# Moving the score and output steps of a fused retention and feed-forward kernel along TensorE's order, and one copy to VectorE

## The chip, the cores and the metric

The kernel runs on one core of a Trainium2 chip. The metric is the device time of one execution in microseconds (us). The profile's names for the engines are kept: PE is TensorE (PEld its weight loads), DVE is VectorE, ACT is ScalarE, POOL is GpSimdE, SP is SyncE, which issues nearly all DMAs. PEclk is the clock that TensorE was granted, 1.00 being full speed.

## The reference: what is computed

Retention for 8 batches, 8 heads, 576 positions and a head size of 64, and then a feed-forward block with a tanh Gelu on the 4608 tokens of 512 features that it gives. Inputs and output are float32.

```python
scores = q @ k.transpose(0, 1, 3, 2) / sqrt(64)
gamma  = 1 - 2.0 ** (-5 - arange(8))            # one decay for each head
rel    = pos[:, None] - pos[None, :]
ret    = scores * where(rel >= 0, gamma ** rel, 0)
x      = (ret @ v).transpose(0, 2, 1, 3).reshape(4608, 512)
h      = x @ w_in                                # 512 x 2048
out    = gelu_tanh(h) @ w_out                    # 2048 x 512
```

## The kernel before

**The work.** The decay is split into a factor for the query's position and one for the key's, applied when q and k are cast to float16 (lines 262 to 297, mostly on GpSimdE). Each batch is cut into four chunks of 128 positions and a tail of 64. Within a chunk the scores are matmuls (`score`, L430) that VectorE masks from PSUM to SBUF (`masks`, L440, its operation at L444). Between chunks a state, k transposed times v (`state`, L454), is summed on VectorE (`scan_halves`, operations at L494, L477 and L472) and cast by ScalarE into the tiles `tbb` and `tbt` (L497 and L505). An output (`outputs`, L526) is the masked scores times v plus the queries times the state. `put` (L561) then copies it, on ScalarE (L569), into `xT`, the feed-forward block's transposed input. The scores and outputs are made of 64x64 matmuls, four of them side by side in the array (`pack`, L401); each has a weight load of its own.

**Blocks.** The feed-forward block runs over nine blocks of 512 tokens, block t for batch t and the ninth for the tails. A block from the third on first multiplies with w_in (`up`, L577, 16 times four matmuls of 128x512, L583, each group followed by a Gelu on ScalarE, L589), and then with w_out: seven products (`prod`, L751, matmuls of 128x256 at L768) in the manner of Strassen, whose sums VectorE and ScalarE take from PSUM (`after`, L775, operations at L782, L821 and L838). Blocks 0 and 1 take their w_in products in halves (L604), and block 1 has these before its own units.

**The order.** The kernel is scheduled by hand. Inside the loop over blocks t, the retention work of batch t + 1 is put between the feed-forward steps. `at(t, u, f)` hangs f behind unit u of block t, and the engines' queues get their instructions in the order in which the steps are then called. In blocks 1 to 7 units 0 to 15 are the w_in steps and units 16 to 29 are the products, two for each (one per half u), in the order 1, 6, 5, 7, 2, 4, 3. Each product is 16 matmuls, 8 for each half. Their PSUM tiles are opA (products 1 and 2), opB (6, 7 and 4) and opC (5 and 3).

The lines that the change touches stand in the planner (L1046 to L1062):

```python
U2 = (21, 23, 28)
at(1, 16, lambda: pack([state(2, 0)]))
...
    s0, o0, o1 = U2 if t == 1 else (11 if t in (2, 3, 4) else 9, 15, 24)
    at(t, s0, lambda b=b, tl=tl: scores(b, tl))
    at(t, o0, lambda b=b, tl=tl: outs(b, 0, tl, (b, 1) if b < B else None))
...
    at(t, o1, lambda b=b: outs(b, 1, None, (b + 1, 0) if b + 1 < B else None))
```

`scores` makes the scores of both halves of batch t + 1, 64 matmuls (and 16 for a pair of tails in blocks 3, 4, 6 and 7), and the four masks. `outs(b, 0)` makes the first half's outputs and, between two changes of the array's use (`TURN`, one small matmul each), the states of the second half; `put` follows in the same step. `outs(b, 1)` makes the second half's outputs and the first states of the batch after. `later` (units 25 and 26 in block 1) hangs the sums of those states on VectorE and their casts on ScalarE. So in block 1 the scores of batch 2 stand between products 5 and 7, the first outputs between products 7 and 2, and the second outputs in the middle of product 3; block 2 follows with its w_in products, which read `xT`.

**PSUM.** There are eight banks, handed out first in, first out by `bank` and `drop` (L61 to L69). The scores hold four, an output step four and one more for the array's changes.

**DMA.** SyncE issues the loads of q, k and v into 16 buffers (`pump`), the stores, and the transposes of the cast k and q into `tt` (L324), which the scores and outputs read. The transposes of a batch stand behind its last cast of q, one block ahead of their use.

Of the kernel before, what the change touches and what calls it, by code (L numbers as in the profile page):

```python
# [20 lines left out]
def kernel(  # L21
# [9 lines left out]
    nc = tc.nc  # L31
# [12 lines left out]
    NPE = 2  # L44
# [22 lines left out]
    def drop(t):  # L67
        spare.append(home.pop(id(t))[0])
# [332 lines left out]
    def pack(*phases, n=None):  # L401
        opened = set()
        for phase in phases:
            if phase is TURN:
                t = ps.tile([128, 512], F32, tag=f"p{n}", name="turn", bufs=1)
                nc.tensor.matmul(t[0:64, 0:4], ident[0:64, 0:64], ident[0:64, 0:4], start=True, stop=True)
                continue
            todo = {x: deque() for x in TILES}
            for jobs in phase:
                for x, *job in jobs:  # L410
                    todo[x].append(job)
            done = dict.fromkeys(TILES, 0)
            while any(todo.values()):
                x = min((x for x in TILES if todo[x]), key=lambda x: done[x])
                t, out, lhsT, rhs = todo[x].popleft()
                k = (id(t), x[1])
                if len(rhs.shape) == 3:
                    out = out.rearrange("p (j t) -> p j t", j=2)
                nc.tensor.matmul(out, lhsT, rhs, start=k not in opened, stop=True, skip_group_check=True)  # L419
                opened.add(k)  # L420
                done[x] += 1
        if n is not None:
            spare.append(n)
# [30 lines left out]
    def state(b, g):  # L454
        a = att[b]
        us = [bank("us") for _ in range(2)]
        out = []
        for o in range(2):
            c = 2 * g + o
            a["U", c] = (us, o)  # L460
            for p in range(HP):
                for r in range(2):
                    i = 256 * o + 64 * p
                    for h in range(2):
                        out.append((
                            (h, r), us[h], us[h][hv(r), i : i + 64], a["k"][hv(h), col(c, p, r)], a["v"][hv(h), col(c, p, row(p, r))]
                        ))
        return out
# [91 lines left out]

    def put(b, g):  # L561
        for h, t in enumerate(att[b].pop(("xs", g))):
            if b >= PAIR:
                nc.scalar.copy(
                    out=xT[:, GM + b - PAIR + h], in_=t.rearrange("p (n x t) -> p n x t", n=HP, x=2)[:, :, 0]
                )
            else:
                g0 = 8 * (b % 2) + 4 * g + h
                nc.scalar.copy(  # L569
                    out=xT[:, g0 : g0 + 4 : 2].rearrange("p g n (t j) -> p g n j t", j=2),  # L570
                    in_=t.rearrange("p (n g j t) -> p g n j t", n=HP, g=2, j=2),
                )
            drop(t)
# [313 lines left out]
    def later(b, c):  # L887
        (scan if b < NPE else scan_halves)(b, c)
        spread(b, c, A.copy)
# [53 lines left out]
    def at(t, u, f, last=False):  # L943
        events.setdefault((t, u, last), []).append(f)
# [75 lines left out]
    def scores(b, tails=None):  # L1020
        w = [score(b, g) for g in range(2)] if b < B else []
        if tails is not None:
            w.append(score(PAIR + tails, 0))
        pack(w)
        if b < B:
            masks(b, 0), masks(b, 1)
        if tails is not None:
            masks(PAIR + tails, 0)

    def outs(b, g, tails=None, ahead=None):  # L1030
        n = spare.popleft()
        first, second, between, todo = [], [], [], []
        if b < B:
            todo.append((b, g))
        if tails is not None:
            todo.append((PAIR + tails, 0))
        for x in todo:
            early, late = outputs(*x)
            first.append(early), second.append(late)
        if ahead is not None:  # L1040
            between.append(state(*ahead))
        pack(first, TURN, between, TURN, second, n=n)
        for x in todo:
            put(*x)

    U2 = (21, 23, 28)  # L1046
    at(1, 16, lambda: pack([state(2, 0)]))
    for c in range(2):
        at(1, 17 + c, lambda c=c: later(2, c))
    for t in range(1, B):  # L1050
        b, tl = t + 1, TP.get(t)
        s0, o0, o1 = U2 if t == 1 else (11 if t in (2, 3, 4) else 9, 15, 24)
        at(t, s0, lambda b=b, tl=tl: scores(b, tl))
        at(t, o0, lambda b=b, tl=tl: outs(b, 0, tl, (b, 1) if b < B else None))
        if b == B:
            continue
        at(t, 25 if t == 1 else 16, lambda b=b: later(b, 2))
        at(t, 26 if t == 1 else 20, lambda b=b: later(b, 3))
        at(t, o1, lambda b=b: outs(b, 1, None, (b + 1, 0) if b + 1 < B else None))
        if b + 1 < B:  # L1060
            for c in range(2):
                at(t + 1, c, lambda c=c, nb=b + 1: later(nb, c))  # L1062
# [119 lines left out]
```

## Time and profile before

| What | Value |
| --- | --- |
| Median of 3 runs | 290.66 us (288.53 to 291.45) |
| The profiled execution | 292.24 us |
| Its span, first to last instruction | 290.5 us |
| Mean granted TensorE clock in it | 0.991 |
| TensorE busy | 275.9 us, 95% |
| VectorE / ScalarE / GpSimdE busy | 195.9 / 169.4 / 114.6 us |
| Read and written in HBM | 36.70 and 9.44 MB |

A line of the timeline gives the start, the time from the first start to the last end of a run of equal instructions, the engine, the line, the operation with the tile that it writes and those that it reads, and how many there are; in brackets the idle time before it and what ended that. Matmuls overlap, so the time of a run reaches a little into the next one: the start of the next run tells better how long one took. "issue" as a cause means that the engine waited for nothing that the profile shows. The columns of a row of stretches are, in this order, the stretch, its length, busy time and (x count) of PE, PEld, DVE, ACT and POOL, the granted clock, the DMA engines' share, and GB/s.

### The profile page before, as it was taken

What the parts mean: (1) busy time and instruction counts of PE and PEld (TensorE: products, weight loads), DVE (VectorE), ACT (ScalarE), POOL (GpSimd) and SP (SyncE); (2) the same over time, 40 slices, a digit from 0 to 9 for tenths busy, and PEclk for the clock granted to TensorE, in tenths of its full rate; (3) what the DMA queues carried; (4) which work ended last, traced back from release to release, by engine and by line L of the source; (5) the groups of instructions that cost most, each with busy time, mean ns of one, the idle gap of its engine ahead of it and who ended that gap; (6) DMA issues with size and microseconds to landing.
All of it is one profiled execution on the core that took longest, in us unless ns stands there. A gap on an engine that the chain in (4) does not pass through costs nothing.

```text
span 290.5 us, 9420 instructions
## 1 busy us (share of the span) xinstructions
PE 275.9 (95%) x3986; PEld 202.8 (70%) x3986; DVE 195.9 (67%) x411; ACT 169.4 (58%) x327; POOL 114.6 (39%) x225
## 2 busy tenths in 40 slices
PE   6789998999799999999999999999999999999993
PEld 2458876888574488548854785478547887887782
DVE  6787988677816573667366746753687867975863
ACT  5387755996237674667466755675566358507800
POOL 4589769971780059205920490049330000000000
PEclk9999999999979999999999999999999999999998
DMA  7999999989979994998999929996982030003013
GB/s 198 305 375 367 380 289 262 278 216 202 237 147 246 248 210 103 224 261 193 197 207 267 208 73 220 260 221 136 234 201 39 2 146 2 2 28 119 0 38 108
DMA packets 127306, 54.09 MB, mean 186 GB/s; under 512 B 93472, under 2 KB 119072, under 8 KB 127264
## 3 DMA queue, kind: packets, MB, share of 16 engines
q1 hardware_dynamic: 126672, 52.97, 78.0%
q8 instruction: 31, 0.51, 0.8%
q10 hardware_dynamic: 592, 0.52, 0.5%
q14 instruction: 11, 0.09, 0.1%
HBM read 36.70 MB, written 9.44 MB: 159 GB/s over the span
## 4 chain that ended last, share of the span: by engine, by line
PE 79%; DMA 10%; POOL 4%; DVE 2%; SPq 1%; issue 1%; ACT 1%; POOLq 0%
PE hp L583 26%; PE opB L768 13%; PE opA L768 10%; PE opC L768 8%; PE hp L604 5%; DMA ld<-in_q_dram 4%; DMA ld<-in_moe_w_out_dram 4%; PE hB L677 3%; PE xs L419 3%; DMA ld<-in_moe_w_in_dram 2%; POOL cq L283 2%; PE hC L677 2%; PE st L419 2%; POOL ck L283 1%; PE us L419 1%; PE opD L768 1%
## 5 line engine op out<-in xcount | busy, mean ns | idle before, releaser
L583 PE MATMUL hp<-xT,w_in_sb 128*128 128x512 f16 x352 | 79.0, 379 | 0.5 <-ACT xT L569 0.5
L589 ACT ACTIVATE gT<-hp 128x512 f16<-128x512 f32 x88 | 51.1, 598 | 30.2 <-PE hp L583 29.7
L768 PEld LDWEIGHTS <-gT 128*128 128x128 f16 x576 | 55.7, 99 | 11.8 <-issue 3.5
L583 PEld LDWEIGHTS <-w_in_sb 128*128 128x128 f16 x352 | 34.0, 98 | 38.4 <-issue 0.6
L768 PEld LDWEIGHTS <-s 128*128 128x128 f16 x432 | 42.1, 98 | 4.9
L768 PE MATMUL opA<-w_out_sb,gT 128*128 128x256 f16 x288 | 37.1, 276 | 2.7 <-issue 1.9
L294 POOL TENSOR_TENSOR ck<-ld,sc 128x128 f16<-128x128 f32 (+1 forms) x72 | 33.7, 494 | 3.1 <-DMA ld<-in_k_dram 3.0
L745 DVE TENSOR_TENSOR s<-gT 128x512 f16<-128x512 f16 x36 | 16.6, 460 | 23.7 <-ACT gT L589 18.0
L1076 POOL COPY gate<-s 128x1 f16<-128x1 f16 x5 | 0.9, 190 | 77.4 <-DVE s L749 77.4
L275 POOL TENSOR_TENSOR cq<-ld,sc 128x256 f16<-128x256 f32 x48 | 29.8, 639 | 0.2 <-DMA ld<-in_q_dram 0.2
L604 PE MATMUL hp<-xT,w_in_sb 128*128 128x256 f16 x256 | 29.4, 273 | 0.4 <-POOL w_in_sb L874 0.3
L768 PE MATMUL opB<-wt,gT 128*128 128x256 f16 x224 | 27.7, 279 | 0.0
L604 PEld LDWEIGHTS <-w_in_sb 128*128 128x128 f16 x256 | 24.4, 98 | 4.3 <-POOL w_in_sb L874 1.1
L569 ACT CAST xT<-xs 128x512 f16<-128x512 f32 x24 | 15.9, 734 | 19.0 <-PE xs L419 19.0
L782 DVE TENSOR_TENSOR k<-k,opB 128x512 f32<-128x512 f32 x17 | 11.6, 685 | 13.1 <-PE opB L768 11.2
L611 ACT ACTIVATE gT<-hp 128x512 f16<-128x512 f32 x32 | 18.4, 603 | 3.4 <-PE hp L604 3.3
L444 DVE TENSOR_TENSOR ret<-st,cm 128x512 f16<-128x512 f32 x24 | 14.9, 684 | 5.5 <-PE st L419 5.5
L746 DVE TENSOR_TENSOR s<-s,gT 128x512 f16<-128x512 f16 x36 | 16.8, 468 | 1.2
L768 PE MATMUL opB<-wt,s 128*128 128x256 f16 x144 | 17.4, 273 | 0.0
L768 PE MATMUL opC<-wt,s 128*128 128x256 f16 x144 | 17.2, 272 | 0.0
L747 DVE TENSOR_TENSOR gT<-gT 128x512 f16<-128x512 f16 x36 | 16.7, 463 | 0.0
L782 DVE TENSOR_TENSOR ost<-k,opB 128x512 f32<-128x512 f32 x6 | 4.1, 689 | 18.2 <-PE opB L768 18.2
(134 smaller groups left out, 438.9 us busy)
## 6 DMA issues: line engine op xcount, KB each, us to landing
ld<-in_q_dram SPq DMA_DIRECT2D x32, 256.0 KB, 5.4
ld<-in_k_dram SPq DMA_DIRECT2D x32, 256.0 KB, 5.4
ld<-in_v_dram SPq DMA_DIRECT2D x32, 256.0 KB, 5.3
out_dram<-ost SPq DMA_DIRECT2D x16, 512.0 KB, 4.2
ld<-in_moe_w_in_dram SPq DMA_DIRECT2D x16, 256.0 KB, 5.6
ld<-in_moe_w_out_dram SPq DMA_DIRECT2D x16, 256.0 KB, 5.7
lt<-in_k_dram SPq DMA_DIRECT2D x8, 128.0 KB, 5.0
lt<-in_q_dram SPq DMA_DIRECT2D x8, 128.0 KB, 4.2
```

The source lines that it names most:

```text
L275: eng.tensor_tensor(out=a[key][:, 1024 * g + 512 * x : 1024 * g + 512 * x + 512].rearrange("p (n l d) -> p l n d", l=2, d=D)[:, y ^ x], in ...
L294: eng.tensor_tensor(out=dh[:, o], in0=x, in1=sc[:, s0, i].unsqueeze(2).to_broadcast(list(x.shape)), op=ALU.mult)
L419: nc.tensor.matmul(out, lhsT, rhs, start=k not in opened, stop=True, skip_group_check=True)
L569: nc.scalar.copy(out=xT[:, g0 : g0 + 4 : 2].rearrange("p g n (t j) -> p g n j t", j=2), in_=t.rearrange("p (n g j t) -> p g n j t", n=HP, ...
L583: nc.tensor.matmul(hp.rearrange("p (g t) -> p g t", t=TL), w_in_sb[:, ct, 128 * fc : 128 * fc + 128], xT[:, o : o + TB // TL, ct, :], star ...
L589: nc.scalar.activation(out=gT[t][:, fc].rearrange("p i n -> p (i n)"), in_=hp, func=AF.Gelu_apprx_tanh)
L604: nc.tensor.matmul(hps[n][:, 256 * x : 256 * x + 256].rearrange("p (g t) -> p g t", t=TL), w_in_sb[:, ct, 128 * (fs[n] + x) : 128 * (fs[n] ...
L611: nc.scalar.activation(out=gT[t][:, f : f + 2, 2 * u : 2 * u + 2, :].rearrange("p f i n -> p f (i n)"), in_=hp.rearrange("p (f n) -> p f n ...
L745: nc.vector.tensor_tensor(out=s["1"], in0=a21, in1=a22, op=ALU.add)
L746: nc.vector.tensor_tensor(out=s["2"], in0=s["1"], in1=a11, op=ALU.subtract)
L747: nc.vector.tensor_tensor(out=a21, in0=a11, in1=a21, op=ALU.subtract)
L768: nc.tensor.matmul(op[tag][:, HD * u : HD * u + HD], lhs(f), rhs[:, f], start=(new and f == 0), stop=(f == NH - 1), skip_group_check=True,)
```

## The change

Three edits. In block 1 the scores of batch 2 are hung behind unit 19 instead of 21, so they stand between products 6 and 5, and the first outputs behind unit 25 instead of 23, so they stand between products 2 and 4. The second outputs stay in the middle of product 3. In `put`, the copy of the second half of the second outputs of batch 2 into `xT` goes from ScalarE to VectorE. In blocks 2, 3 and 4 the scores are hung behind unit 10 instead of 11.

What follows for the queues: TensorE's instructions are the same 3986 pairs in another order. On VectorE the order of all others stays, with the one copy between the sum that takes product 4 and the one that takes product 3. On ScalarE the copy of opA (L838) now stands ahead of the two copies of the first outputs instead of behind them, and one of the last two copies is gone. GpSimdE's and SyncE's orders stay.

```diff
@@ put(b, g)
         for h, t in enumerate(att[b].pop(("xs", g))):
+            cp = nc.vector.tensor_copy if (b, g, h) == (NPE, 1, 1) else nc.scalar.copy
             if b >= PAIR:
...
                 g0 = 8 * (b % 2) + 4 * g + h
-                nc.scalar.copy(
+                cp(
                     out=xT[:, g0 : g0 + 4 : 2].rearrange("p g n (t j) -> p g n j t", j=2),
                     in_=t.rearrange("p (n g j t) -> p g n j t", n=HP, g=2, j=2),
                 )
@@ the planner
-    U2 = (21, 23, 28)
+    U2 = (19, 25, 28)
...
-        s0, o0, o1 = U2 if t == 1 else (11 if t in (2, 3, 4) else 9, 15, 24)
+        s0, o0, o1 = U2 if t == 1 else (10 if t in (2, 3, 4) else 9, 15, 24)
```

## The prediction

> **What bounds the kernel now.** I read the page first, for engine shares, the clock row and the DMA queues.
>
> ```profile
> span 290.5 us, 9420 instructions
> PE 275.9 (95%) x3986; PEld 202.8 (70%) x3986; DVE 195.9 (67%) x411; ACT 169.4 (58%) x327; POOL 114.6 (39%) x225
> ...
> PEclk9999999999979999999999999999999999999998
> ...
> q8 instruction: 31, 0.51, 0.8%
> ...
> PE 79%; DMA 10%; POOL 4%; DVE 2%; SPq 1%; issue 1%; ACT 1%; POOLq 0%
> ```
>
> TensorE is busy for 95% of the span and is 79% of the chain, so only its pauses and its slow stretches can be won. Its clock dips in one slice before the end, the thirteenth. Queue q8 brings 31 packets of 0.51/31 MB, 16 KB each; TensorE issues 3986 matmuls and 3986 weight loads, 7972 instructions, and 7972/31 is 257. So a packet is a page of some 256 TensorE instructions. Next, TensorE's waits, of which these two lie in block 1, and its stretches around the dip (a row gives the stretch, busy time and count of each engine, then PEclk, DMA share, GB/s):
>
> ```profile
> PE opA L768 <- issue: 1.9, 1, 1.9
> PE hp L583 <- ACT xT L569: 0.5, 1, 0.5
> ```
>
> ```profile
> 43.00:47.00 4.00, 2.79 (x85) 2.11 (x82) 3.21 (x6) 3.44 (x6) 4.00 (x5) 1.00 1.15 287
> 77.85:79.73 1.88, 0.01 (x2) 0.01 (x1) 1.60 (x5) 0.77 (x2) 0.22 (x2) 1.00 1.29 247
> 80.30:83.70 3.40, 3.40 (x19) 2.42 (x17) 0.19 (x1) 1.72 (x5) 3.40 (x8) 0.50 0.73 169
> ```
>
> TensorE stands still for 1.9 us with no engine named, and 0.6 us later runs 3.4 us at half clock. A pause of 1.21 in 4.0 us (first row) cost no clock. Then TensorE's order of time in block 1 and at the start of block 2 (start, us, engine, line, tiles, count, idle before):
>
> ```profile
> 69.82 1.91 PE L768 MATMUL opB<-wt,s 128*128 128x256 f16 x16
> 71.57 1.91 PE L768 MATMUL opC<-wt,s 128*128 128x256 f16 x16
> 73.41 0.74 PE L419 MATMUL st<-tt 64*64 64x64 f16 x64
> ...
> 74.08 1.92 PE L768 MATMUL opB<-wt,gT 128*128 128x256 f16 x16
> 75.93 0.31 PE L419 MATMUL xs<-tt,tbb 64*64 64x64 f16 x12
> ...
> 77.25 0.61 PE L768 MATMUL opA<-w_out_sb,gT 128*128 128x256 f16 x4
> 79.73 2.21 PE L768 MATMUL opA<-w_out_sb,gT 128*128 128x256 f16 x12 [1.87 <-issue]
> 81.73 2.89 PE L768 MATMUL opB<-wt,gT 128*128 128x256 f16 x16
> 84.46 1.04 PE L768 MATMUL opC<-w_out_sb,s 128*128 128x256 f16 x8
> 85.43 0.32 PE L419 MATMUL xs<-tt,tbb 64*64 64x64 f16 x16
> ...
> 86.51 1.05 PE L768 MATMUL opC<-w_out_sb,s 128*128 128x256 f16 x8
> 88.02 10.52 PE L583 MATMUL hp<-xT,w_in_sb 128*128 128x512 f16 x48 [0.46 <-ACT xT L569]
> 98.47 0.74 PE L419 MATMUL st<-tt 64*64 64x64 f16 x64
> ```
>
> The pause falls after four of the sixteen matmuls of one product, whose operands are no different from the first four's: not a wait for data. Last, what moved on the DMA engines in 73.8 to 76.8, 76.8 to 78.2 and 80.8 to 82.5 us:
>
> ```profile
> q1 hardware_dynamic: 2339, 0.72, 130.4%
> ```
>
> ```profile
> q8 instruction: 1, 0.02, 5.7%
> ```
>
> ```profile
> q8 instruction: 1, 0.02, 5.9%
> ```
>
> In the first stretch the data queue takes more than the engines' whole time and no page comes; one comes in 76.8 to 78.2, TensorE resumes 1.5 us after that stretch ends, and the next comes in 80.8 to 82.5. I read the pause as TensorE out of instructions. Small matmuls eat pages fast: the scores are 64 pairs (weight load and matmul), 128 instructions in 74.08 - 73.41 = 0.67 us, and an output step 90 pairs, 180 in 77.25 - 75.93 = 1.32 us, while a product's 32 take 1.75 us. The instruction that waited follows 4 pairs (8), the output step (180) and a product (32), 220 in all; 256 back from it lies 92 instructions into the scores, at 73.41 + 0.67 x 92/128 = 73.9 us. If the page then needed was asked for there, its **latency** was 79.73 - 73.9 = 5.8 us, and TensorE had used up its page by 77.7.
>
> [...]
>
> **The change part by part.** All times are on the clock of this profiled execution: 292.24 us, span 290.5 and 1.74 around it. That is 1.58 over the median of the three runs shown (290.66), 0.79 over the slowest.
>
> *Scores two products forward, outputs one back (block 1).* The same instructions, reordered; SyncE's and GpSimdE's orders stay, so no DMA is passed. TensorE's new order from 71.57: scores 0.67, products 5, 7 and 2 (1.75, 1.75, 1.85 with the 0.1 that precedes a burst), outputs from 77.6 to 78.9, product 4 to 80.7, half of product 3 (84.46 to 85.43 is 0.97) to 81.6, second outputs (1.08) to 82.7, and 0.88 to 83.6. Page edges stay where they are in the count of instructions. The first now comes 124 of 128 into the scores, 71.57 + 0.65 = 72.2; the second 156 of 180 into the outputs, 77.6 + 1.14 = 78.7. Between them are 6.5 us instead of 3.8, more than the latency of 5.8. The pause goes: 79.73 less the 77.69 at which a fifth matmul at 0.11 would have begun, 2.04 us. The half clock goes with it: 12 matmuls took 2.00 and 16 took 2.73, against 1.31 and 1.75, so 1.67 us. **-3.71 us.**
>
> *What is late next.* The third edge comes 184 of 196 into the second outputs, about 82.5, only 3.8 us after the second; by the old order it was 6.6. No row shows a latency so short: the page asked for at 79.73 came by 82.5, and with the 1.5 to resume that is 4.3. The wait is between 0 (latency 3.8) and 2.0 (5.8). I take 4.3, the nearest row, since the DMA share falls from 1.29 to 0.73 just there: **+0.5 us**, too short for a half clock.
>
> The moved steps' own waits, with the rows that hide them:
>
> ```profile
> 64.35 3.10 SPq L324 DMA_TRANSPOSE tt<-cq  x1
> ```
>
> ```profile
> 86.00 3.31 SPq L324 DMA_TRANSPOSE tt<-cq  x1
> ```
>
> ```profile
> DMA to landing us min/median/max: 4.4/5.9/6.5
> ```
>
> ```profile
> 77.30 1.32 ACT L569 CAST xT<-xs 128x512 f16<-128x512 f32 x2 [4.05 <-PE xs L419]
> ...
> 82.46 0.41 ACT L497 CAST tbb<-ts 128x256 f16<-128x256 f32 x1
> 82.77 0.41 ACT L505 CAST tbb<-ws 128x256 f16<-128x256 f32 x1
> 83.07 0.41 ACT L497 CAST tbb<-ts 128x256 f16<-128x256 f32 x1
> ...
> 86.65 1.32 ACT L569 CAST xT<-xs 128x512 f16<-128x512 f32 x2 [2.87 <-PE xs L419]
> ```
>
> ```profile
> 84.66 0.69 DVE L782 TENSOR_TENSOR ost<-k,opB 128x512 f32<-128x512 f32 x1 [4.18 <-PE opB L768]
> 87.59 0.69 DVE L782 TENSOR_TENSOR ost<-k,opC 128x512 f32<-128x512 f32 x1 [2.24 <-PE opC L768]
> ```
>
> The scores need the turned queries: issued at 64.35, landed by 70.9 at the slowest, before 71.57; zero, and every 0.1 us later would be a 0.1 us pause. The second outputs need ScalarE's third state copy. ScalarE now copies opA first (done 78.2), then the outputs (78.9 to 80.2, by the 1.32), then states at 0.31 apart: the third ends at 81.2, TensorE asks at 81.6. Zero, with 0.4 of cover; past that TensorE waits.
>
> *Last copy on VectorE.* TensorE's last matmul of block 1 ends near 86.51 + 0.88 = 87.39 and block 2 begins at 88.02, after ScalarE's two copies in a row (1.32). With one on each engine they end at 86.65 + 0.73, 87.4. VectorE stands idle from 85.35 to 87.59, and its 512-column operations on PSUM take 0.69, so it hides the copy: 0.63 becomes 0.05. From nothing gained (VectorE late) to 0.63; I take **-0.58**. If VectorE were late, the sums of product 3 queue behind it, whose output nobody waits for soon.
>
> *Blocks 2 to 4.* Scores start one unit earlier (four 512-column matmuls: 48 in the 10.45 from 88.02 to 98.47, so 0.87). In block 2 the turned queries, issued at 86.00, land by 92.5 at the slowest; the scores come at 98.47 - 4.3 - 0.87 = 93.3: zero, with 0.8 of cover. No wait of TensorE lies between 88.1 and 285 us other than the one above, and a shorter path to masks that nothing awaits gains nothing. It gives the pages more time, though:
>
> ```profile
> 157.43:162.19 4.76, 4.76 (x152) 2.65 (x140) 4.66 (x11) 2.64 (x5) 0.00 (x0) 1.00 1.32 236
> ```
>
> Counted on from the pause, pages 9 and 10 begin at 157.43 and 162.19, with scores and outputs between: 4.76 us and no pause, but a latency of 5.8 would have cost 1.0. The change adds some 0.8 there. Between 0 and -1.0; zero here, since this execution did not pay it.
>
> *Sum.* 292.24 - 3.71 - 0.58 + 0.5 = 288.4. This execution is 1.58 over the median and over every plain run, which may be a longer pause (not kept) or a cost of recording spread over the span (which the new kernel's plain runs lack too). The fastest plain run, 288.53, is just 292.24 - 3.71: a run without the pause. I split the 1.58 and take half off, 0.8: **287.6 us** for plain runs, and the same 0.8 off each rival.
>
> **The rivals.** *The pause isn't a late page, or stays.* [...] Against: 16 KB per 257 instructions, the packet that ends just before TensorE resumes. Only the copy gains: 292.24 - 0.58 = 291.7 recorded, 290.9 plain.
>
> *The pause moves.* The third edge has 3.8 us, no more than the second had; at the old latency it waits 2.0 and brings the half clock (1.67) again, so 288.4 - 0.5 + 3.7 = 291.6 recorded, 290.8 plain. For it: the near-equal distance. Against: the DMA engines are at 0.73 there, not 1.3.
>
> *Slower: pages come later still.* With latency L the first wait is L - 6.5 and the second L - 3.8, with 1.67 of half clock; together they pass the 4.29 won at 2L = 12.9, L = 6.5. At 7.5 it is 1.0 + 3.7 + 1.67 = 6.4, or 2.1 over the 292.24: 294.3 recorded, 293.5 plain. For it: both requests are now made before 79.7, while the DMA engines are full (130.4% in 73.8 to 76.8). Against: the 5.8 was measured under that very load, and the second request's packet meets the lighter one.
>
> **How the numbers follow.** Pause gone, short or no wait at the next page: 0.65, time 287.6, own range 286.6 to 288.9 (below it no wait, 0.5, and half of the 1.0 of blocks 3 and 4; above it most of the wait's further 1.5). Pause moved in full: 0.15. Pause stays: 0.12. Slower: 0.08, near 293.5. The range reaches from 286.6 to 290.9: it takes in the first three cases and leaves out the slower one and the outer ends of the others. What a measurement of this kernel can tell from no change is about 1%, 2.9 us (the three runs spread over 2.92). Faster by over 1% is below 287.75, somewhat more than half of the first case: 0.40. Slower by over 1%, above 293.57: half of the slow case and a little of the moved pause, 0.06. The rest, 0.54, lies within.
>
> **What would show it.** Right: no "issue" wait of TensorE near 77 to 80, the clock row without its dip, no wait for xT at the start of block 2, which begins near 83.6 to 84.5 instead of 88.02. A wait in the second outputs, just past 82, would be the third edge. Wrong: a half clock elsewhere in block 1, a pause in front of the scores (turned queries late) or of the second outputs (state copies late), or VectorE's copy ending after the last matmul of block 1.

## The result, and the profile after

| What | Before | After |
| --- | --- | --- |
| Median (lowest to highest) of 20 runs each | 290.49 us (288.53 to 292.50) | 288.55 us (287.34 to 291.06) |
| The profiled execution | 292.24 us | 288.71 us |
| Its mean granted TensorE clock | 0.991 | 1.000 |

The changed kernel takes 0.9938 of the time before, with a 95% interval of 0.9915 to 0.9961: between 1.1 and 2.5 us less. That is a gain that can be measured, and it lies within the 1% that the prediction called about the same. A ratio and its interval are worked out from the runs in the faster of two states and not from the medians, so the quotient of two medians can differ from it a little. From here on, the line numbers of the changed kernel are one higher than before (L768 is now L769), because the edit in `put` adds a line.

First the page of the profiled execution after: span, engines, the clock in 40 slices, and the chain by engine.

```profile
span 287.0 us, 9420 instructions
PE 274.5 (96%) x3986; PEld 202.1 (70%) x3986; DVE 196.5 (68%) x412; ACT 169.3 (59%) x326; POOL 115.3 (40%) x225
...
PEclk9999999999999999999999999999999999999999
...
PE 81%; DMA 9%; DVE 3%; POOL 3%; issue 1%; ACT 1%; SPq 0%; POOLq 0%; DVEq 0%
```

The dip in the clock row is gone, and one copy has gone from ACT's count to DVE's. TensorE's waits still have one row without a cause, which now stands in the outputs; the wait for xT at the start of block 2 is no longer among them:

```profile
PE xs L419 <- issue: 1.1, 1, 1.1
```

TensorE's order of time in block 1 (start, us, engine, line, tiles, count, idle before):

```profile
71.77 0.74 PE L419 MATMUL st<-tt 64*64 64x64 f16 x64
72.44 1.92 PE L769 MATMUL opC<-wt,s 128*128 128x256 f16 x16
74.19 1.91 PE L769 MATMUL opB<-wt,gT 128*128 128x256 f16 x16
75.94 1.91 PE L769 MATMUL opA<-w_out_sb,gT 128*128 128x256 f16 x16
77.78 0.28 PE L419 MATMUL xs<-tt,tbb 64*64 64x64 f16 x10
...
78.77 1.92 PE L769 MATMUL opB<-wt,gT 128*128 128x256 f16 x16
80.53 1.04 PE L769 MATMUL opC<-w_out_sb,s 128*128 128x256 f16 x8
81.49 0.32 PE L419 MATMUL xs<-tt,tbb 64*64 64x64 f16 x16
...
82.07 0.44 PE L419 MATMUL xs<-ret,cv 64*64 64x64 f16 x25
83.58 0.25 PE L419 MATMUL xs<-ret,cv 64*64 64x64 f16 x7 [1.08 <-issue]
83.77 1.05 PE L769 MATMUL opC<-w_out_sb,s 128*128 128x256 f16 x8
84.69 0.61 PE L584 MATMUL hp<-xT,w_in_sb 128*128 128x512 f16 x2
```

Product 2, where TensorE stood still for 1.87 us, now runs its 16 matmuls through (75.94), and the next burst follows at full clock. In place of that pause TensorE stops once, for 1.08 us, in the second outputs, seven matmuls before their end: the place that the prediction gave the third page edge (about 82.5). Block 2 begins at 84.69 instead of 88.02, a little past the 83.6 to 84.5 that the prediction gave, with no wait ahead of it. From the end of product 6 (71.57 before, 71.77 after) to the start of block 2 it was 16.45 us and is now 12.92: 3.53 less, as much as the whole profiled execution lost (292.24 - 288.71 = 3.53). Blocks 2 to 4 gave nothing in it.

The DMA queues after, in 78.5 to 80.9, then in 80.9 to 82.3 us:

```profile
q1 hardware_dynamic: 1781, 0.58, 106.9%
```

```profile
q1 hardware_dynamic: 1033, 0.28, 99.4%
q8 instruction: 1, 0.02, 5.4%
```

The edge before lies near 78.5. For 2.4 us after it the data queue fills the DMA engines and no page comes; one comes in the next 1.4 us, and TensorE goes on 1.3 us after that stretch. From edge to resumption it is 83.58 - 78.5 = 5.1 us. This row of stretches (stretch, length, busy time and count of PE, PEld, DVE, ACT, POOL, then clock, DMA share, GB/s) shows the load around it:

```profile
78.50:82.52 4.02, 4.00 (x147) 3.40 (x135) 3.49 (x7) 2.60 (x6) 4.02 (x9) 1.00 1.06 232
82.52:83.58 1.06, 0.00 (x0) 0.00 (x0) 0.00 (x0) 0.00 (x0) 0.72 (x3) 1.00 0.69 179
```

TensorE had 4.0 us for a page that took 5.1; the DMA share was 1.06 until the pause and fell to 0.69 only within it. ScalarE's and VectorE's order of time show the covers (start, us, engine, line, tiles):

```profile
77.89 0.59 ACT L839 COPY ost<-opA 128x512 f32<-128x512 f32 x1 [4.59 <-PE opA L769]
78.82 1.33 ACT L570 CAST xT<-xs 128x512 f16<-128x512 f32 x2 [0.35 <-PE xs L419]
...
80.60 0.42 ACT L497 CAST tbb<-ts 128x256 f16<-128x256 f32 x1
...
83.86 0.73 ACT L570 CAST xT<-xs 128x512 f16<-128x512 f32 x1 [1.72 <-PE xs L419]
```

```profile
83.91 0.73 DVE L570 CAST xT<-xs 128x512 f16<-128x512 f32 x1 [1.61 <-PE xs L419]
84.85 0.69 DVE L783 TENSOR_TENSOR ost<-k,opC 128x512 f32<-128x512 f32 x1 [0.22 <-PE opC L769]
```

The third state copy is done at 81.0, before TensorE asks at 81.49. The last two copies into `xT` run side by side and end at 84.6, as the last products do.

### The profile page after: what moved, and what is told of

It reads as the page before. It is cut to its first block, busy times and chain, and to the rows that moved or that the text cites. A ratio compares the mean times of both kernels' runs of the same rounds, so it can differ in the third digit from the quotient of the medians.

```text
span 287.0 us, 9420 instructions
## 1 busy us (share of the span) xinstructions
PE 274.5 (96%) x3986; PEld 202.1 (70%) x3986; DVE 196.5 (68%) x412; ACT 169.3 (59%) x326; POOL 115.3 (40%) x225
## 4 chain that ended last, share of the span: by engine, by line
PE 81%; DMA 9%; DVE 3%; POOL 3%; issue 1%; ACT 1%; SPq 0%; POOLq 0%; DVEq 0%
PE hp L584 26%; PE opB L769 13%; PE opA L769 10%; PE opC L769 9%; PE hp L605 5%; DMA ld<-in_moe_w_in_dram 4%; PE hB L678 3%; PE xs L419 3%; DMA ld<-in_q_dram 3%; DMA ld<-in_moe_w_out_dram 2%; PE hC L678 2%; PE st L419 2%; POOL cq L283 1%; PE us L419 1%; PE opD L769 1%; PE tr L312 1%
## 5 line engine op out<-in xcount | busy, mean ns | idle before, releaser
L769 PEld LDWEIGHTS <-gT 128*128 128x128 f16 x576 | 55.0, 98 | 8.7 <-issue 1.2
L769 PEld LDWEIGHTS <-s 128*128 128x128 f16 x432 | 42.0, 98 | 4.9
L769 PE MATMUL opA<-w_out_sb,gT 128*128 128x256 f16 x288 | 36.2, 273 | 0.7 <-ACT w_out_sb L875 0.5
L769 PE MATMUL opB<-wt,gT 128*128 128x256 f16 x224 | 26.8, 273 | 0.0
L769 PE MATMUL opB<-wt,s 128*128 128x256 f16 x144 | 17.4, 273 | 0.0
L769 PE MATMUL opC<-wt,s 128*128 128x256 f16 x144 | 17.2, 273 | 0.0
L750 DVE TENSOR_TENSOR s<-gT,s 128x512 f16<-128x512 f16 x36 | 16.0, 457 | 0.0
```

What stands on the lines that cost most here:

```text
L750: nc.vector.tensor_tensor(out=s["4"], in0=a12, in1=s["2"], op=ALU.subtract)
L769: nc.tensor.matmul(op[tag][:, HD * u : HD * u + HD], lhs(f), rhs[:, f], start=(new and f == 0), stop=(f == NH - 1), skip_group_check=True,)
```

## The experiments

My theory: TensorE ran out of instructions, because a page asked for at one page edge (one in some 256 instructions, by the 31 packets for 7972) takes 4 to 6 us under the data load (4.3 and 5.8 us counted in the trace before, 5.1 in the one after), and two edges stood closer than that; moving steps pulls the two apart. Rivals: the pause belongs to the steps themselves or their data, and moves with them whatever the edges do; or the gain is the copy's or that of blocks 2 to 4. In the shortened diffs below a minus is the kernel before, or the changed kernel where it says so.

### Each part alone

**The moves in block 1 alone.**

```diff
-    U2 = (21, 23, 28)
+    U2 = (19, 25, 28)
```

> Only block 1's scores and outputs move; the last copy stays on ScalarE and blocks 2 to 4 stay. Late page: the pause of 1.9 us and the half clock near 77 to 84 us are gone, a pause of about 1 us stands in the second outputs just past 82 us (1.08 in the changed kernel), and TensorE still waits 0.5 us for xT at the start of block 2. So 3.7 less the 1.1: some 2.6 us under a run of the kernel before that has the pause, ratio about 0.993. Rival, the copy and not the moves brings the gain: ratio 1.000, the pause stays.

Measured: 289.15 us beside 290.14, ratio 0.9977 (0.9944 to 1.0011). TensorE's waits by cause, and the two waits near the block's end in its order of time:

```profile
PE xs L419 <- issue: 1.1, 2, 0.6
...
PE hp L583 <- ACT xT L569: 0.4, 1, 0.4
```

```profile
82.47 0.25 PE L419 MATMUL xs<-ret,cv 64*64 64x64 f16 x7 [0.64 <-issue]
...
84.11 2.10 PE L583 MATMUL hp<-xT,w_in_sb 128*128 128x512 f16 x9 [0.42 <-ACT xT L569]
```

What follows: the old pause is gone without the copy, and the new one stands at the same seven matmuls as in the changed kernel, here 0.64 us. The wait for xT is still there. A second pause, of 0.42 us, stands in block 4 (in 157.9 to 159.2 us, at a DMA share of 1.28), by the count at a page edge. The median gained less than expected, and its interval takes in no change.

**The copy alone.**

```diff
+            cp = nc.vector.tensor_copy if (b, g, h) == (NPE, 1, 1) else nc.scalar.copy
...
-                nc.scalar.copy(
+                cp(
```

> Only the last copy of outputs goes to VectorE. Both theories: no wait for xT at the start of block 2, VectorE's copy takes 0.73 us (as in the changed kernel) beside ScalarE's. Late page: the pause with issue as its cause stays after the fourth opA matmul near 78 us, 1 to 2 us long, since no instruction of TensorE moved. Gain 0.5 us, which the time of one run can't show but the timeline can.

Measured: 288.18 us in a single execution. Waits:

```profile
PE opA L769 <- issue: 0.8, 1, 0.8
```

```profile
76.58 0.61 PE L769 MATMUL opA<-w_out_sb,gT 128*128 128x256 f16 x4
78.04 1.48 PE L769 MATMUL opA<-w_out_sb,gT 128*128 128x256 f16 x12 [0.84 <-issue]
...
84.05 4.27 PE L584 MATMUL hp<-xT,w_in_sb 128*128 128x512 f16 x19
```

What follows: with the old order the pause stands after the same four matmuls of product 2. But it is 0.84 us, and twelve matmuls take 1.48, so there is no half clock: the pause of 1.87 with its half clock was not what every execution pays. The wait for xT is gone, as predicted.

**Blocks 2 to 4 alone.**

```diff
-        s0, o0, o1 = U2 if t == 1 else (11 if t in (2, 3, 4) else 9, 15, 24)
+        s0, o0, o1 = U2 if t == 1 else (10 if t in (2, 3, 4) else 9, 15, 24)
```

> Only the scores of blocks 2 to 4 go one unit forward. No change in the profile on TensorE beyond their place: no wait of TensorE appears or goes in blocks 2 to 4, the pause in block 1 stays. Ratio 0.999 to 1.001. If runs without a recording pause in blocks 3 and 4 too (4.7 us between page edges there, some 0.8 more with the change), the median falls by up to 1 us, ratio 0.997.

Measured: 289.79 us beside 290.14, ratio 0.9976 (0.9939 to 1.0012). In its order of time:

```profile
78.91 1.49 PE L768 MATMUL opA<-w_out_sb,gT 128*128 128x256 f16 x12 [1.02 <-issue]
...
85.46 0.81 PE L583 MATMUL hp<-xT,w_in_sb 128*128 128x512 f16 x3 [0.47 <-ACT xT L569]
```

What follows: block 1, untouched, shows a pause of 1.02 us and no half clock, the second such execution. The interval takes in no change, but also the 0.997 that I gave for pauses spared in blocks 3 and 4; a closer comparison stands further down.

### The page edges, with the steps left in place

**Edges moved in the kernel before.** 108 pairs of tiny matmuls ahead of all work make every later edge fall 216 instructions earlier in the work. They read zeros, and nobody reads what they write.

```diff
+    zt = const.tile([128, 64], F16, name="zt")
+    nc.vector.memset(zt, 0.0)
+    def tiny(n):
+        ts = [bank("tiny") for _ in range(2)]
+        for i in range(n):
+            r, c = TILES[i % 4]
+            nc.tensor.matmul(ts[r][hv(c), 0:4], zt[hv(r), 0:64], zt[hv(r), 0:4], start=True, stop=True)
+        for t in ts:
+            drop(t)
+    tiny(108)
```

> The kernel before, with 108 pairs of tiny matmuls (64x64 weights of zeros, 4 columns, read by nobody) put ahead of everything, where TensorE waits for its first operands. No step is moved; each page edge of TensorE's instructions falls 216 instructions earlier in the work. Late page: edges then lie 40 instructions after the old ones less one page, the shortest time between two edges in the dense stretches is about 4.3 us instead of 3.8 and none lies in block 1 under 4.7, so the pause and the half clock near 78 us are gone without any reordering: 2 to 3.7 us less than before, ratio 0.988 to 0.993. Rival, the pause comes from the order of the steps or from what the fifth opA matmul waits for: the pause stays after the fourth opA matmul, ratio 1.00 or a little above.

Measured: 289.74 us beside 290.14, ratio 0.9987 (0.9954 to 1.0020). Its three longest waits, and product 2 in its order of time:

```profile
PE xs L531 <- ACT tbb L524: 1.7, 2, 1.0
PE tr L322 <- DVE ck L293: 1.6, 1, 1.6
PE tiny L253 <- DVE zt L162: 1.1, 1, 1.1
...
```

```profile
78.22 1.92 PE L778 MATMUL opA<-w_out_sb,gT 128*128 128x256 f16 x16
```

What follows: the steps of block 1 stand in the old order, and the pause is gone (16 matmuls in one run, no wait without a cause). So in this execution it went with the edges and not with the steps or their data. The time was missed: the median fell by 0.4 us where I expected 2 to 3.7, and its interval takes in no change. Why is open. The scores that began at 73.41 in the kernel before begin at 74.38 here, but in the other traces of the old order they begin anywhere from 72.74 to 74.47, so a cost of the tiny matmuls at the start is not shown. Two of the twelve executions (292.38 and 293.17 us) have a mean clock of 0.994, as low as the kernel before with its half clock; no trace shows where they lost it.

**Edges moved in the changed kernel.** The same with `tiny(52)`, 104 instructions.

> The changed kernel with 52 pairs of tiny matmuls ahead of everything, so that each page edge falls 104 instructions earlier in the work; no step is moved. Late page: two edges now enclose nothing but the first outputs of block 3 (124 pairs), 1.8 us apart, so a new pause with issue as its cause stands in product 1 of block 3, a few matmuls after those outputs, 2.5 to 4 us long, probably with a half clock behind it; the pause in block 1 stays at about 1 us but inside the states of the second outputs. 3 to 5 us slower than the changed kernel: 291 to 294. Rival, order or operands cause the pause: no wait in block 3, the pause stays seven matmuls before the end of the second outputs, time within 1 us of the changed kernel.

Measured: 289.49 us in a single execution; the kernel before on that chip had 290.5 (289.46 to 294.64). In its order of time, first block 1, then block 3:

```profile
83.65 0.28 PE L429 MATMUL us<-cv,ck 64*64 64x64 f16 x10 [0.60 <-issue]
...
125.75 3.40 PE L594 MATMUL hp<-xT,w_in_sb 128*128 128x512 f16 x15
...
129.08 0.28 PE L429 MATMUL xs<-tt,tbb 64*64 64x64 f16 x10
```

The DMA queues in 127.7 to 129.1 us of it:

```profile
q8 instruction: 1, 0.02, 5.7%
```

What follows: the pause in block 1 moved with the edge, out of the last output matmuls and into the states before them: counted through the two orders of time, it stands exactly 52 pairs earlier in the work, as many as were put ahead. The larger pause that I expected in block 3 did not come, and so the 291 to 294 us were missed. One page came in 127.7 to 129.1 us, none in 129.1 to 131, and TensorE ran without a wait through the edge at the end of the w_in matmuls (about 129.1) and through the next, 1.8 us later. So I take the page for that next edge to have been asked for before TensorE's execution reached the first, and a latency counted from there as too long in this place; how far ahead the request went out, no trace shows.

### The load on the DMA engines

**Big packets.** Batch 3's 12 loads read rows of w_out in place of q, k and v (same bytes, 2 KB packets), so batch 3's result is left out.

```diff
-        if b < NPE or key == "q":
+        if b == 3:
+            nc.sync.dma_start(out=t, in_=moe_w_out[128 * c : 128 * c + 128, :])
+        elif b < NPE or key == "q":
```

> The kernel before, with the twelve loads of batch 3 (the ones in flight during block 1) replaced by loads of as many bytes of w_out in rows of 2 KB; batch 3's result is left wrong by that. If the page is late because its packet waits behind the many small packets of these loads, the DMA share between 73 and 77 us falls below 1 and the pause after the fourth opA matmul shrinks below 0.5 us or goes. If the latency doesn't hang on that load, the pause stays at 1 to 2 us.

Measured: 291.55 us in a single execution. In its order of time, and the stretch ahead:

```profile
80.96 1.48 PE L770 MATMUL opA<-w_out_sb,gT 128*128 128x256 f16 x12 [2.04 <-issue]
```

```profile
73.00:78.50 5.50, 5.36 (x187) 4.45 (x185) 5.22 (x10) 1.10 (x4) 5.50 (x11) 1.00 1.04 385
```

What follows: the lighter load did not come about. The share fell from 1.34 (72.0 to 76.8 us of the kernel before) to 1.04, which still fills the DMA engines, at 385 GB/s, and the pause stayed, at 2.04 us. So it does not need small packets: of the 1162 packets in this stretch only 128 are under 2 KB.

**No loads.** The same 12 loads replaced by GpSimdE memsets; batch 3's result is left out again.

```diff
-        if b < NPE or key == "q":
+        if b == 3:
+            nc.gpsimd.memset(t, 0.0)
+        elif b < NPE or key == "q":
```

> The kernel before, with the twelve loads of batch 3 replaced by GpSimdE memsets of the same tiles; batch 3's result is left wrong by that. TensorE's stream and page edges are those of the kernel before. If the page is late because the DMA engines are full of data, there is little data in 73 to 78 us now, the packet starts within 1.5 us of the edge and the pause after the fourth opA matmul is gone or under 0.3 us. If the latency of 5 us is the queue's own, the pause stays at 1 us or more. The run above with rows of 2 KB could not tell, since its loads kept the engines as full (share 1.04).

Measured: 289.50 us in a single execution; the kernel before on that chip had 290.63 (288.68 to 293.50). Product 2, and the stretch ahead:

```profile
77.85 1.92 PE L770 MATMUL opA<-w_out_sb,gT 128*128 128x256 f16 x16
```

```profile
73.00:78.00 5.00, 4.86 (x182) 3.99 (x181) 4.78 (x8) 0.50 (x2) 5.00 (x10) 1.00 0.01 3
```

The DMA queues in 75.4 to 76.4 us of it:

```profile
q8 instruction: 1, 0.02, 5.8%
```

What follows: with edges and steps in place and the DMA engines empty (share 0.01 instead of 1.3), the pause is gone. The edge, 92 instructions into scores that begin at 74.01, lies near 74.5, and the packet came 0.9 to 1.9 us after it; in the kernel before it came in 76.8 to 78.2, 2.9 to 4.3 us after an edge at 73.9. Together with the moved edges this shows the cause: a page asked for 3.8 us ahead of its use comes late under the load of the data queue, 5.8 us from edge to resumption at a share of 1.30. One wait of 0.4 us without a cause is left in this execution, in an output outside block 1, like the 0.42 that the moves alone show in block 4.

### Where the outputs belong

**First outputs at unit 24, at unit 23 (where they stood), and at 23 again.** All else as in the changed kernel.

```diff
-    U2 = (19, 25, 28)
+    U2 = (19, 24, 28)
```

At unit 23 the line is `U2 = (19, 23, 28)`.

> The changed kernel with the first outputs half a product earlier (unit 24). Late page: the first two edges are 5.7 us apart and the next two 4.6, where the latencies in block 1 have been 4.6 to 5.9: the pause in the second outputs falls from 1.1 to between 0 and 0.5 us. Ratio to the kernel before 0.991 to 0.993. Rival: the pause stays at 1.1 us, ratio 0.994.

> The changed kernel with the first outputs where they were (unit 23), so that in block 1 only the scores move. Late page: the edges are 5.4 and 5.1 us apart, the most even of the three, so neither wait is over 0.5 us and most executions have none. Ratio to the kernel before 0.990 to 0.993, the best of the three. Rival: no difference from the changed kernel, 0.994.

> The version with the first outputs at unit 23 once more, beside the next two on the same chip. Late page: no wait with issue as its cause over 0.5 us in block 1, ratio 0.988 to 0.993.

Measured: 287.64 us beside 290.50, ratio 0.9897 (0.9870 to 0.9924), at unit 24; 288.27 beside the same, 0.9905 (0.9876 to 0.9935), at 23; 287.96 beside 290.63, 0.9898 (0.9847 to 0.9949), at 23 again. Unit 24's scores in its order of time, and TensorE's wait in the repeated run of unit 23:

```profile
72.88 0.73 PE L419 MATMUL st<-tt 64*64 64x64 f16 x64 [0.56 <-DMA tt<-cq]
```

```profile
PE xs L419 <- issue: 0.3, 1, 0.3
```

What follows: with only the scores moved, the edges stand about 5 us apart each, and the pauses are 0 or 0.3 us, with both outputs in their old places. In the run at 24 the scores waited 0.56 us for the turned queries, the wait against which the prediction had found a cover of less than 0.7 us.

**Outputs at 23, and blocks 2 to 4 back at unit 11.**

```diff
-        s0, o0, o1 = U2 if t == 1 else (10 if t in (2, 3, 4) else 9, 15, 24)
+        s0, o0, o1 = U2 if t == 1 else (11 if t in (2, 3, 4) else 9, 15, 24)
```

> The same, with the scores of blocks 2 to 4 back at unit 11. Block 1's pauses no longer blur the comparison. If the move in blocks 2 to 4 is worth something only by giving the pages more time (edges 4.7 us apart without it, 5.5 with it), some executions pause in block 3 or 4: 0.2 to 1.0 us over the version with unit 10. If not, no difference within 0.3 us.

Measured: 287.95 us beside 290.63, ratio 0.9890 (0.9844 to 0.9936), against 287.96 with unit 10 on the same chip. The medians show nothing for the third edit. The traces leave a little open: of the six with these scores at unit 11 and no tiny matmuls ahead, two have a pause of about 0.4 us outside block 1, of the six with unit 10 none.

**Outputs at 23, and the copy back on ScalarE.**

```diff
-            cp = nc.vector.tensor_copy if (b, g, h) == (NPE, 1, 1) else nc.scalar.copy
+            cp = nc.scalar.copy
```

> The same, with the last copy of outputs back on ScalarE. TensorE waits 0.5 us for xT at the start of block 2 again, so 0.5 to 0.6 us over the version with the copy on VectorE, ratio 0.002 higher.

Measured: 288.53 us beside 290.63, ratio 0.9934 (0.9910 to 0.9959). In its order of time:

```profile
84.06 2.10 PE L584 MATMUL hp<-xT,w_in_sb 128*128 128x512 f16 x9 [0.47 <-ACT xT L570]
```

What follows: the wait for xT is back. By medians on one chip the copy is worth 288.53 - 287.96 = 0.57 us (by the ratios 1.0), though the two intervals overlap. And this kernel against the one before gives what moving the scores is worth in the median, the old pause above all: 290.63 - 288.53 = 2.10 us (by the interval 1.2 to 2.6).

## Why the prediction came near, and where its sum was off

**Cause and place: right.** The pause is a late page. It went when the edges moved and no step did, it went when the load did and no edge moved, and after the change it stood at the next edge, within 0.1 us of where the count put it. The rival that the pause stays is out. Moved edges and missing loads rest on one trace each, but all four traces of the old order with full DMA engines and the edges in place have the pause, and neither of these two has it.

The size of a page agrees with the runs: 7972 instructions come in 31 packets, 257 for each, and counted from the end of product 6 the instruction that waits in the trace after (the 636th) stands 255 behind the one that waited in the trace before (the 381st). Nearly all of the some 30 edges of a trace show no wait. At none, one or two of them the crossing showed, at 0.3 to 2.0 us, within bursts of small matmuls or four matmuls behind one; in four of these places the DMA share ahead of the pause or around it was read, and it was 1.04 to 1.30.

**The pause and its half clock, -3.71: right for the profiled execution, too large for the median.** The trace after shows both gone (the dip stood in the twelfth of the 40 slices, not the thirteenth). But that execution of the kernel before was among the longest: only one of its 20 runs took longer. Of the 54 executions of the kernel before that ran beside the experiments, only 10 have a mean clock of 0.994 or lower, and these took 291.36 to 294.64 us (two others took 292.48 and 293.14 at nearly full clock); half a clock for 3.4 us is worth 1.7 of 290, or 0.006 of the mean. None of the 20 runs after lies below 0.996. So most executions of the kernel before (44 of these 54) show no half clock of that length, and without one the pause was 0.84 and 1.02 us in two old-order traces above, 2.04 in the one with big packets. The table gives the prices in time, from the start of the first burst after product 6 to block 2:

| Trace | Product 6 done, us | Block 2 begins, us | Between |
| --- | --- | --- | --- |
| Before | 71.57 | 88.02 | 16.45 |
| Before, big packets | 72.63 | 87.51 | 14.88 |
| Blocks 2 to 4 alone | 71.60 | 85.46 | 13.86 |
| Before, edges moved | 72.54 | 85.20 | 12.66 |
| Before, no loads | 72.17 | 84.83 | 12.66 |
| Outputs at 23, copy on ScalarE | 71.82 | 84.06 | 12.24 |
| Outputs at 23 | 71.08 | 82.78 | 11.70 |
| Changed kernel | 71.77 | 84.69 | 12.92 |

The pause with its half clock was worth 16.45 - 12.66 = 3.79, without it 1.20 and 2.22. How it is spread over executions without a trace stays open.

**What the sum left out.** The order with the scores moved is 12.66 - 12.24 = 0.42 us shorter, with no pause in either. The prediction gave the first outputs the 1.32 us that they took before; they took 0.99 in the changed kernel (77.78 to 78.77). In the kernel before, the states inside them stopped until VectorE had done the scores' last mask (start, us, engine, line, tiles):

```profile
73.90 2.48 DVE L444 TENSOR_TENSOR ret<-st,cm 128x512 f16<-128x512 f32 x4 [0.49 <-PE st L419]
76.08 0.80 PE L419 MATMUL us<-cv,ck 64*64 64x64 f16 x32
76.44 0.33 PEld L419 LDWEIGHTS <-ck 64*64 64x64 f16 x29 [0.25 <-issue]
```

They went on at 76.44, 0.06 us after the masks' end at 76.38, and in the runs with edges moved and without loads the 32 states took the same 0.80 us. Presumably they waited for the PSUM bank that this mask frees; no run tests it. With the scores further ahead the masks are done at 75.85 in the changed kernel, 2 us before the states, and that stop is gone (29 of the 32 states in 0.45 us).

**The new wait, +0.5: mis-sized.** It was 1.08 us, and 12.92 - 11.70 = 1.22 from burst to burst. I had taken 4.3 us from edge to resumption, on the ground that the DMA share falls to 0.73 there. It fell only afterwards: the page was now asked for at 78.5 instead of 79.7, the share was 1.06 until the pause, and the page took 5.1 us. Counted in the same way, it was 4.6 in the run with the moves alone, where the wait was 0.64. The other bound, 5.8, was that of the rival of a pause that moves in full, 2.0 us with a half clock; it held for half: the pause moved and shrank. In the median its price would be the difference between the ratios 0.9938 and 0.9890 to 0.9905, which is 0.3 to 0.5% or 1.0 to 1.4 us and includes the trace's figures; but these kernels were not run side by side. That such a wait would cost no clock was right (it is 1.00 in the 1.11 us behind the wait), but the row given for it was misread: its 1.21 us without work are two waits, of 0.49 and 0.73.

**The copy, -0.58: right.** The wait of 0.46 is gone, VectorE's copy ran while it would have been idle, the table gives 12.24 - 11.70 = 0.54, and the median 0.57.

**Blocks 2 to 4, zero: right in the median,** 287.95 against 287.96 us. Some executions may be spared the 0.4 us that two traces show outside block 1.

**The covers.** The states' copies were ready 0.5 us before they were asked for (0.4 predicted). The turned queries held in the trace after and failed by 0.56 us in one execution at unit 24, where the scores stand in the same place; so that cover is sometimes used up, in the changed kernel too, I suppose, though no trace of it shows that.

**The sum, 288.4 recorded and 287.6 plain.** For a profiled execution like the first, 288.4 stood against 288.71. That it came so near is in part luck: the wait was 0.7 too small, and the 0.42 of the new order was missing (3.79 + 0.42 + 0.54 - 1.22 = 3.53 measured, 3.71 + 0.58 - 0.5 = 3.79 forecast). The step that failed is the half of the 1.58 us that I took off as a cost of recording. The changed kernel's profiled 288.71 is close to its median of 288.55, and of the eight experiments with several runs the profiled execution lies below the median in five and above it in three. So no such cost shows: the 1.58 fits the longer pause and the half clock of an execution at the upper end. With nothing taken off, and the terms as the medians and the table give them, it is 290.5 - 2.1 - 0.57 + 1.2 = 289.0, against 288.55. The sum for the profiled execution came out right because its start, 292.24, and its price of the pause, 3.71, belong to the same execution; the 0.8 taken off is nearly all of the 0.95 us by which the forecast lies below the median. The own range of this case, 286.6 to 288.9, holds the median.

**A better version.** With the scores moved and the first outputs left at unit 23, or put at 24, the ratio was 0.9890 to 0.9905 in four measurements, against 0.9938 for the changed kernel. Their intervals overlap with its own, and they were not run beside it, so a further gain of about 1 us is likely but not shown. Moving the first outputs back is what brings the second edge too near the third (4.0 us of work between them in the changed kernel, for a page that took 5.1).

## What to carry to other kernels

Where the profile names no cause for an idle bottleneck engine ("issue") amid instructions whose operands are ready, count its instructions since the last such edge: divide its total by the packets of the instruction queue (7972 by 31 here), and see whether two edges stand closer in time than a page takes to come (4.6 to 6.0 us in the block 1 of these traces). Bursts of small instructions use up pages fastest (128 in the 0.67 us of the scores here, 32 in the 1.75 us of a product), so spread them until the edges are evenly apart, and move no more of them than that needs. Before a pause of one trace is put into a sum, see where that execution stands among the runs; a difference between a trace and the median is first of all a sign of an unusual execution.

## What the runs showed of the hardware

- From the edge at which a page is asked for to the resumption of TensorE it took, counted through the instructions of each trace with a pause in block 1, 4.6 to 6.0 us: 5.8 at a DMA share of 1.30 (before), 5.1 at 1.06 (changed kernel) and 6.0 at 1.04 (big packets), and 4.6 to 5.5 in the five others, whose share was not read. In the two traces above in which the packet was looked for, TensorE resumed 1.3 and 1.5 us after the stretch in which it came. At a share of 0.01 the packet came 0.9 to 1.9 us after the edge, and there was no pause.
- The half clock does not follow the length of a pause alone. In the kernel before, 1.88 us without work were followed by 3.4 us at 0.50; the 2.04 us of the run with big packets were followed by twelve matmuls in 1.48 us, at full clock. The twelve that followed the pause in the kernel before took 2.21 us. What else decides it, no run shows.
- In one stretch of 128x512 matmuls (0.22 us each) a page came before TensorE's execution reached the edge (changed kernel with edges moved: packet in 127.7 to 129.1 us, edge by the count at about 129.1), and TensorE did not wait at the next edge.
